# An attention and expert kernel: expert layers on two batches at once by seven block products in place of eight, with all weight conversion in the first two batches

## The chip, the cores and the metric

One core of a Trainium2 chip. The time is the device time of one execution in microseconds (us). The kernel before has a median of 1721.91 us over 3 runs (1719.16 to 1723.12).

## What is computed

Attention with a mixing of the heads ahead of the softmax and behind it, then four matrix products per token ("experts"); 8 batches, 12 heads, 448 positions, head size 64:

```python
scores = scale * np.matmul(q, k.transpose(0, 1, 3, 2))
scores = np.einsum('bhij,hg->bgij', scores, w_pre)
attn = softmax(scores)
attn = np.einsum('bhij,hg->bgij', attn, w_post)
x = np.matmul(attn, v)            # as [8*448 tokens, 768]
a, b = x @ w1, x @ w2             # 768 -> 1024
out = ((a * b) @ w3) @ w_out      # 1024 -> 1024 -> 768
```

The four weights arrive as 64-bit floating-point words.

## The kernel before, in words

**Steps.** The program is written out as one loop over `n` from 0 to 365 (`run`, lines 526 to 591). A step is ten positions of a batch with all twelve heads, 120 rows of 448 scores; a batch is 45 steps, so that there are 360. Within a step, in this order: the load of the scores of step n+4 (`fetch`), what was put off from the step before (`do_later`: stores and weight loads on SP's one DMA queue), the softmax of n (`softmax`: a minimum `mn` on DVE, the exponential `e` on ACT), the scaling of the second mixing matrix for n-1 (`scale`, `w2` on DVE), the split of the scores of n+2 into a high part `rh` (DVE) and a low part `rl` (POOL), scores of the next batch (`qk`), the weight conversion, half of the step's share of expert matmuls (`advance`), the second mixing (`post`, tile `pso`, copied to `mt`), the product with v (`av`, tile `psa`), the other half, and the first mixing of n+1 (`mix`, tile `psm`).

**Two parts.** Operands of the split products are held in the type fp32r, and a product is made of three matmuls: high with high, high with low, low with high (`PAIRS`). Of every operand a high part is copied by ACT and a low part is made by POOL as the difference (`two_parts`, lines 101 to 104; `el` on line 386).

**Weights.** `converting` takes 72 pieces of 64-bit words (`cs`, 384 KB each), turns them into float32 by four DVE instructions and one of ACT (`to_f32`, lines 91 to 98) and splits them. First come 40 pieces of w_out and w3, whose product (`folding`, 384 matmuls into `psf`) is made in steps 16 to 48 and stored in `w34_d`; then 32 pieces of w1 and w2 (`unit_jobs`), which are used at once for batch 0 and stored in `w_d` for the others, 16 stores of 768 KB.

**Experts.** `expert_atoms` takes one batch: for each of 8 blocks of 128 columns and w1, w2 a group of 18 matmuls (line 373) into bank 6 or 7, their product on DVE (`em`), its two parts (`eh`, `el`), then 6 groups of 24 matmuls with the folded weight (line 398). That is 432 matmuls of 128 by 448 a batch and 3456 in all. They are given out to the steps by `shares`: 288 to steps 53 to 106, 432 to every 45 steps from there, the rest (739) behind the loop. Weights come as "units" of 768 or 512 KB, two ahead (`w_ahead`), seven ahead behind the loop. The attention output of a batch stays in SBUF, split into `xh` and `xl` straight from PSUM.

Of the kernel before, what the change touches and what calls it, by code (L numbers as in the profile page):

```python
# [16 lines left out]
IB = 10  # L17
# [3 lines left out]
GB = 15  # L21
# [4 lines left out]
LATE = 2 * NB + GB + 2  # L26
PAIRS = ((0, 0), (0, 1), (1, 0))

# [3 lines left out]
class Kernel:  # L32
# [52 lines left out]
    def to_f32(self, s, name):  # L85
# [11 lines left out]
        x = self.cs.tile([128, CW], F32, tag="x", name=f"cx{name}")[:, :n]  # L97
# [8 lines left out]
    def converting(self, jobs):  # L106


        words, made = [], None
        jobs = list(jobs)  # L110
        for n in range(-2, len(jobs) + 1):
            if n + 2 < len(jobs):
                src = jobs[n + 2][0]
                words.append(self.words(src, f"{self.n_words}"))
                self.n_words += 1
            if made:
                jobs[n - 1][1](made)
                made = None
            if 0 <= n < len(jobs):
                made = self.to_f32(words.pop(0), f"{self.n_made}")  # L120
                self.n_made += 1
            yield

# [102 lines left out]
    def post(self, n):  # L226
# [8 lines left out]
        copy = nc.scalar.copy if n < LATE else nc.vector.tensor_copy  # L235
# [16 lines left out]
    def av(self, b, a, g):  # L252
# [10 lines left out]
        if g % 3 == 2:  # L263
            if b not in self.xs:
                pool = self.xp[b % 2]
                self.xs[b] = [pool.tile([128, K1, S], F32R, tag=f"x{t}", name=f"x{t}{b}") for t in "hl"]
            h, l = (x[:, g - 2:g + 1, cols] for x in self.xs[b])
            q = self.psa[:, :, :W]
            self.ends.append((5, lambda: nc.scalar.copy(h, q)))
            self.soon.append((5, lambda: nc.vector.tensor_tensor(l, q, h.bitcast(F32), op=ALU.subtract)))  # L270
# [4 lines left out]
    def fold_jobs(self):  # L275
        self.fo = self.fp.tile([128, KF, 2, DM], F32R, tag="o", name="fo", bufs=1)
        for k in range(KF):
            for q in range(2):
                src = self.w_src[3][k * 128:(k + 1) * 128, 2 * q * DH:2 * (q + 1) * DH]
                hi, lo = (self.fo[:, k:k + 1, t, q * DH:(q + 1) * DH] for t in range(2))  # L280
                yield src.rearrange("p (a n) -> p a n", a=1), lambda x, hi=hi, lo=lo: self.two_parts(x, hi, lo)
        w3 = self.w_src[2].rearrange("(k p) f -> p k f", p=128)
        for f in range(KF):
            for k in (slice(0, 3), slice(3, 6), slice(6, 8)):
                yield w3[:, k, f * 256:(f + 1) * 256], lambda x, f=f, k=k: self.fold_part(x, f, k)
# [5 lines left out]

    def folding(self):
        nc = self.nc
        for f in range(KF):
            for half in range(2):
# [7 lines left out]
                z = self.fp.tile([128, 3, 2, 128], F32R, tag="z", name=f"fz{half}_{f}")  # L303
                q = p.rearrange("p (d c) -> p d c", c=128)
                dst = self.w34_d[half * 3:(half + 1) * 3, :, f].rearrange("d p t c -> p d (t c)")

                def low(z=z, q=q, dst=dst):
                    nc.vector.tensor_tensor(z[:, :, 1], q, z[:, :, 0].bitcast(F32), op=ALU.subtract)
                    self.later.append(lambda: nc.sync.dma_start(dst, z.rearrange("p d t c -> p d (t c)").bitcast(F32)))

                self.ends.append((6 + half, lambda z=z, q=q: nc.scalar.copy(z[:, :, 0], q)))
                self.soon.append((6 + half, low))
# [3 lines left out]
    def units(self):  # L316
        return [u for b in range(B) for u in
                [(w, f, 0) for f in range(KF) for w in range(2)] + [(3, d, q) for d in range(K1) for q in range(2)]]

    def load_unit(self):  # L320
        w, f, q = self.unit_list[self.n_loaded]
        t = self.wp.tile([128, K1, 2, 128], F32R, tag="w", name=f"wu{self.n_loaded}")
        if w < 2:
            self.nc.sync.dma_start(t.bitcast(F32), self.w_d[w][f])
        else:
            h = KF // 2
            t = t[:, :h]
            self.nc.sync.dma_start(t.bitcast(F32), self.w34_d[f][:, q * h:(q + 1) * h])
# [4 lines left out]
    def unit_jobs(self):  # L333

        h = K1 // 2
        for w, f, _ in self.unit_list[:2 * KF]:
            src = self.w_src[w].rearrange("(k p) f -> p k f", p=128)
            for q in range(2):
                yield src[:, q * h:(q + 1) * h, f * 256:(f + 1) * 256], lambda x, w=w, f=f, q=q: self.unit_part(x, w, f, q)

    def unit_part(self, x, w, f, q):
        h = K1 // 2
        if q == 0:
            self.unit = self.wp.tile([128, K1, 2, 128], F32R, tag="w", name=f"wu{self.n_loaded}")
            self.loaded.append(self.unit)
            self.n_loaded += 1
        t = self.unit
        self.two_parts(x, *(t[:, q * h:(q + 1) * h, i] for i in range(2)))
        if q:
            self.later.append(lambda: self.nc.sync.dma_start(self.w_d[w][f], t.bitcast(F32)))  # L350

    def next_unit(self):

        t = self.loaded.pop(0)
        while 2 * KF <= self.n_loaded + self.n_asked < len(self.unit_list) and \
                len(self.loaded) + self.n_asked < self.w_ahead:
            self.n_asked += 1
            self.later.append(self.load_unit)
        return t

    def experts(self):
        for b in range(B):
            yield from self.expert_atoms(b)

    def expert_atoms(self, b):
        nc, xs, hs = self.nc, self.xs.pop(b), []
        for f in range(KF):
            for i in range(2):
                w = self.next_unit()
                p = self.bank(6 + i, f"eg{b}_{f}_{i}")[:, :S]  # L370
                for k in range(K1):
                    for t, (x, y) in enumerate(PAIRS):
                        nc.tensor.matmul(p, w[:, k, x], xs[y][:, k],  # L373
                                         start=(k == 0 and t == 0), stop=(k == K1 - 1 and t == 2))
                        yield
                if i == 0:
                    a = self.sp.tile([128, S], F32, tag="a", name=f"ea{b}_{f}", bufs=1)
                    self.ends.append((6, lambda a=a, p=p: nc.scalar.copy(a, p)))
            m = self.sp.tile([128, S], F32, tag="m", name=f"em{b}_{f}", bufs=1)
            self.ends.append((7, lambda m=m, a=a, p=p: nc.vector.tensor_tensor(m, a, p, op=ALU.mult)))  # L380
            h = self.hp.tile([128, S], F32R, tag=f"h{f}", name=f"eh{b}_{f}")
            l = self.hp.tile([128, S], F32R, tag=f"l{f}", name=f"el{b}_{f}")

            def parts(m=m, h=h, l=l):
                nc.scalar.copy(h, m)  # L385
                nc.gpsimd.tensor_tensor(l, m, h.bitcast(F32), op=ALU.subtract)  # L386

            self.soon.append((None, parts))
            hs.append((h, l))
        self.do_ends()  # L390
        self.do_soon()
        for d in range(K1):
# [263 lines left out]
```

## Time and profile before

| what | value |
|---|---|
| median of 3 runs | 1721.91 us (1719.16 to 1723.12) |
| the profiled execution | 1720.68 us, its span 1718.9 us |
| TensorE (PE), busy | 1648.0 us, 96% |
| DVE, POOL, ACT, busy | 935.8, 752.0, 723.6 us |
| moved by DMA | 416.51 MB, 242 GB/s over the span |
| steps 0 to 19 | up to 122.4 us |
| steps 20 to 99 | 122.4 to 451.4 us |
| steps 100 to 358 | 451.4 to 1549.7 us |
| what is left | 1549.7 to 1718.9 us |

A step is counted from its first mixing (`psm`, line 199) on TensorE; the borders are the starts of those matmuls. PE's busy time counts the modelled ends of pipelined matmuls. ACT is ScalarE, DVE VectorE, POOL GpSimd; an idle time is named with what ended it.

### The profile page before, as it was taken

Reading aid. Unit: us, or ns where it says so; the run is one execution under the profiler, and the core shown is the slowest. Engines: PE = TensorE matmul, PEld = TensorE weight load, DVE = VectorE, ACT = ScalarE, POOL = GpSimd, SP = SyncE. Lnnn points to the kernel's source line nnn. Section 1 sums busy time; section 2 is a strip of 40 time slices with the busy share of each in tenths; the row PEclk is TensorE's granted clock in tenths of the full one; section 3 lists DMA queues with packets and bytes.
Section 4 is the critical chain, followed back from the end, with each engine's and each line's share of the span. In section 5 each row is a group of like instructions: output and inputs, shape, how many; then the busy total and the mean of one; then the engine's idle time right before and its main releaser. Section 6 shows DMA issues by size and latency. Waiting matters only on the chain.

```text
span 1718.9 us, 30630 instructions
## 1 busy us (share of the span) xinstructions
PE 1648.0 (96%) x10872; PEld 1487.2 (87%) x10872; DVE 935.8 (54%) x2502; ACT 723.6 (42%) x1734; POOL 752.0 (44%) x668
## 2 busy tenths in 40 slices
PE   3889998999999999999999999999999999999999
PEld 1579997788889999899989999899998999998998
DVE  4958667778745555455545555555555555552000
ACT  3867656667643443343433434334433322221010
POOL 1666555667643544444543445345544333231010
PEclk7999999999999999999999999999999999999999
DMA  7979768999888777787778877787768755765764
GB/s 258 294 251 288 244 216 257 289 302 293 265 245 273 241 243 225 240 264 244 247 219 264 253 234 235 246 257 248 244 214 269 226 190 174 236 192 219 263 203 130
DMA packets 186822, 416.51 MB, mean 242 GB/s; under 512 B 17582, under 2 KB 130990, under 8 KB 186670
## 3 DMA queue, kind: packets, MB, share of 16 engines
q1 hardware_dynamic: 186670, 414.57, 76.4%
q8 instruction: 85, 1.39, 0.3%
q14 instruction: 67, 0.55, 0.1%
HBM read 307.54 MB, written 106.95 MB: 241 GB/s over the span
## 4 chain that ended last, share of the span: by engine, by line
PE 72%; DMA 2%; DVE 1%; ACT 0%; issue 0%; POOL 0%; SPq 0%; DVEq 0%; ACTq 0%
PE eg L373 25%; PE eo L398 13%; PE pso L231 13%; PE psa L261 7%; PE psm L199 4%; PE psm L200 3%; PE psm L201 3%; PE psq L164 3%; PE psq L165 3%; DMA wu<-w_d 2%; DVE mn L208 0%; DVE cx L98 0%; DVE ca L95 0%; DVE ca L96 0%; ACT st L169 0%
## 5 line engine op out<-in xcount | busy, mean ns | idle before, releaser
L192 POOL TENSOR_TENSOR rl<-r,rh 120x448 fp32r<-120x448 f32 x360 | 413.2, 1148 | 697.4 <-DVE rh L191 330.5
L211 ACT ACTIVATE e<-psm,mn 120x448 f32<-120x448 f32 x360 | 228.5, 635 | 671.6 <-DVE sa L220 562.5
L373 PE MATMUL eg<-xh,wu 128*128 128x448 f32 x1536 | 478.4, 375 | 4.9 <-ACT wu L103 4.5
L208 DVE TENSOR_REDUCE mn<-psm 120x1 f32<-120x448 f32 x360 | 224.6, 624 | 422.5 <-PE psm L201 422.2
L231 PEld LDWEIGHTS pso<-w,e 120*112 120x112 f32 (+1 forms) x2880 | 348.0, 178 | 47.2 <-ACT mt L237 31.8
L231 PE MATMUL pso<-w,e 120*112 120x120 f32 (+1 forms) x2880 | 360.9, 268 | 15.9 <-ACT mt L237 14.9
L373 PEld LDWEIGHTS eg<-xh,wu 128*128 128x128 f32 x1536 | 284.1, 189 | 28.7 <-ACT wu L103 5.2
L373 PE MATMUL eg<-xl,wu 128*128 128x448 f32 x768 | 284.4, 370 | 0.0
L398 PE MATMUL eo<-eh,wu 128*128 128x448 f32 x768 | 233.9, 375 | 11.0 <-DMA wu<-w_d 11.0
L237 DVE COPY mt<-pso 112x480 f32<-112x480 f32 (+1 forms) x253 | 165.4, 654 | 137.3 <-PE pso L231 136.4
L169 ACT COPY st<-psq 112x448 f32<-112x448 f32 x336 | 173.1, 526 | 16.2 <-DMA raw_d<-st 13.2
L398 PEld LDWEIGHTS eo<-eh,wu 128*128 128x128 f32 x768 | 143.2, 190 | 23.6 <-DMA wu<-w_d 12.9
L261 PE MATMUL psa<-mt,v 112*64 112x150 f32 (+1 forms) x2304 | 156.9, 292 | 1.9 <-DVE xl L270 1.3
L199 PE MATMUL psm<-rh,wph 120*120 120x448 f32 x360 | 139.6, 388 | 18.1 <-DVE rh L191 18.1
L373 PEld LDWEIGHTS eg<-xl,wu 128*128 128x128 f32 x768 | 145.0, 189 | 11.0 <-issue 0.2
L261 PEld LDWEIGHTS psa<-mt,v 112*64 112x64 f32 x2304 | 143.6, 137 | 7.8 <-DVE xl L270 1.6
L191 DVE CAST rh<-r 120x448 fp32r<-120x448 f32 x360 | 146.0, 406 | 0.4 <-DMA r<-raw_d 0.4
L398 PE MATMUL eo<-el,wu 128*128 128x448 f32 x384 | 142.9, 372 | 0.0
L201 PE MATMUL psm<-rl,wph 120*120 120x448 f32 x360 | 132.7, 369 | 0.3 <-POOL rl L192 0.2
L200 PE MATMUL psm<-rh,wpl 120*120 120x448 f32 x360 | 132.5, 368 | 0.0
L386 POOL TENSOR_TENSOR el<-em,eh 128x448 fp32r<-128x448 f32 x64 | 73.8, 1153 | 129.5 <-ACT eh L385 129.5
L164 PE MATMUL psq<-kk,qh 128*112 128x448 f32 x336 | 124.7, 371 | 3.3 <-ACT st L169 3.0
(51 smaller groups left out, 1900.9 us busy)
## 6 DMA issues: line engine op xcount, KB each, us to landing
wu<-w_d SPq DMA_DIRECT2D x112, 768.0 KB, 5.9
r<-raw_d SPq DMA_DIRECT2D x352, 210.0 KB, 3.3
raw_d<-st SPq DMA_DIRECT2D x168, 392.0 KB, 4.1
wu<-w_d SPq DMA_DIRECT2D x96, 512.0 KB, 5.4
v<-v SPq DMA_DIRECT2D x144, 224.0 KB, 4.9
kq<-kq SPq DMA_DIRECT2D x42, 672.0 KB, 7.1
cs<-w SPq DMA_DIRECT2D x32, 384.0 KB, 6.5
w_d<-wu SPq DMA_DIRECT2D x16, 768.0 KB, 5.6
```

The lines of the kernel that those rows point to most:

```text
L164: nc.tensor.matmul(p, qh[:, cols], kk, start=True, stop=False)
L169: copy(st[:, c % 2], p)
L192: nc.gpsimd.tensor_tensor(rl[:K], r[:K], rh[:K].bitcast(F32), op=ALU.subtract)
L199: nc.tensor.matmul(p[:K, :S], self.wph[:K, :K], rh[:K], start=True, stop=False)
L200: nc.tensor.matmul(p[:K, :S], self.wpl[:K, :K], rh[:K], start=False, stop=False)
L201: nc.tensor.matmul(p[:K, :S], self.wph[:K, :K], rl[:K], start=False, stop=True)
L208: nc.vector.tensor_reduce(mn[:K], p[:K, :S], axis=AX.X, op=ALU.min)
L211: nc.scalar.activation(e[:K], p[:K, :S], AF.Exp, bias=mn[:K], scale=-1.0, accum_out=sm[:K])
L231: nc.tensor.matmul(p[:, j, :, :w], e[:K, j * JT:(j + 1) * JT], w2[:K, :, :w], start=True, stop=True)
L261: nc.tensor.matmul(self.psa[rows, g % 3, :W], v[:, j, rows], mt[:, j, 2 * g + s, :W], start=(j == 0), stop=(j == NJ - 1))
L373: nc.tensor.matmul(p, w[:, k, x], xs[y][:, k], start=(k == 0 and t == 0), stop=(k == K1 - 1 and t == 2))
L398: nc.tensor.matmul(p, w[:, k % (KF // 2), x], hs[k][y], start=(k == 0 and t == 0), stop=(k == KF - 1 and t == 2))
```

## The change

Two batches 2p and 2p+1 are taken as one problem. The operand is cut into quarters: 11 and 21 are the upper and lower half of the features of the first batch, 12 and 22 of the second. Instead of eight products of a weight quarter with an operand quarter there are seven products of sums (Strassen's scheme in the form with the fewest additions), numbered 1 to 7 and made in the order 1, 6, 7, 5, 3, 2, 4.

- A pair has 11 groups of columns. Of w1 and w2 there are 8 groups of 9 matmuls, of the folded weight 3 groups of 12, each seven times: 756 matmuls a pair, 3024 in all.
- The weight sums are made once: for each of 12 sets of four quarters POOL does four additions or subtractions (`quarter`, 48 in all), and the seven results are split (ACT and POOL) in a `g` buffer and stored, 84 stores of 384 KB (`staged`). `do_micro` lets at most three of these pieces go into a step.
- The pieces of w1 and w2 are now taken alternately with those of w3, and all 72 are done by about step 90. Folding is spread over steps 22 to 91. No expert matmul runs before step 103; pair p is worked on in the 90 steps from 90(p+1)+13, the last pair behind the loop.
- The attention output goes from PSUM through ACT to DRAM (`x_d`, 48 stores) and comes back as quarters in float32 (96 loads of 224 KB). Operand sums are subtractions on DVE (`prepare`), 40 a pair; each product's operands are split by ACT and POOL, 70 splits a pair where there were 16 for two batches.
- Results are gathered from PSUM by one ACT copy and seven DVE additions per group (`gather`). The product a*b moves from DVE to POOL (`mult`, 64 in all). All `mt` copies are ACT's; before, DVE made those of steps from 107 on.
- Units are 384 or 512 KB, three ahead.

The core of the diff:

```diff
-LATE = 2 * NB + GB + 2
+NS = 51
+ORDER = (1, 6, 7, 5, 3, 2, 4)
...
+    def quarter(self, name, have, q, x, new, put):
+        def part(product, x):
+            self.micro.append(lambda: put(product, x))
+        def add(out, a, b, op):
+            self.micro.append(lambda: self.nc.gpsimd.tensor_tensor(out, a, b, op=op))
...
+    def staged(self, x, name, store):
+        if self.n_staged > 2:
+            self.do_later()
+        t = self.zp.tile([128, 3, 2, 128], F32R, tag="g", name=name, bufs=4)
+        self.two_parts(x, t[:, :, 0], t[:, :, 1])
...
-        copy = nc.scalar.copy if n < LATE else nc.vector.tensor_copy
+        copy = nc.scalar.copy
...
-            self.ends.append((5, lambda: nc.scalar.copy(h, q)))
-            self.soon.append((5, lambda: nc.vector.tensor_tensor(l, q, h.bitcast(F32), op=ALU.subtract)))
+            def leave():
+                nc.scalar.copy(x, q)
+                self.later.append(store)
+            def store():
+                nc.sync.dma_start(dst, x)
...
+            def split():
+                hi, lo = (self.take(f"{p}{name}_{m}_{k}", F32R) for p in ("eh", "el"))
+                nc.scalar.copy(hi, x)
+                nc.gpsimd.tensor_tensor(lo, x, hi.bitcast(F32), op=ALU.subtract)
...
+                if to:
+                    nc.vector.tensor_tensor(a[out], a[to[0]], p, op=ALU.add)
+                else:
+                    nc.scalar.copy(a[out], p)
...
+                def mult():
+                    x, y = acc[f, 0][q], acc[f, 1][q]
+                    nc.gpsimd.tensor_tensor(x, x, y, op=ALU.mult)
...
+            for k in range(nk):
+                for t, (x, y) in enumerate(PAIRS):
+                    nc.tensor.matmul(p, w[:, k, x], ops[m, k][y],
+                                     start=(k == 0 and t == 0), stop=(k == nk - 1 and t == 2))
...
-        FOLD, SWITCH, E_AT = 16, NB + 5, NB + 8
-        E_1, E_2 = 2 * KF * K1 * 3, K1 * KF * 3
+        FOLD, F_END, SWITCH = GB + 7, 2 * NB + 2, 2 * NB + 7
+        E_1 = 7 * 3 * (2 * K1 // 2 * KF // 2 + KF // 2 * K1 // 2)
...
-        share = shares(FOLD, SWITCH - 1, F_N) | shares(E_AT, LATE, E_1)
-        for n in range(LATE, N - 1, NB):
-            share |= shares(n, min(n + NB, N), int((E_1 + E_2) * min(1, (N - n) / NB)))
+        share = shares(FOLD, F_END, F_N)
+        for pair in range(B // 2 - 1):
+            first = 2 * NB * (pair + 1) + 13
+            last = min(first + 2 * NB, N + 6)
+            share |= shares(first, last, E_1 if last < N else E_1 - 60)
...
+            self.do_micro(3)
```

What stands on POOL in the second batch, in the kernel before: each `rl` is one step; `wu` is the low part of a piece of w1 or w2, `ql` and `kk` are the low parts of q and k.

```order
L192 TENSOR_TENSOR rl_5096<-r_4968,rh_5095 120x448
L104 TENSOR_TENSOR wu_5045<-cx_5054,wu_5045 128x3x128
L192 TENSOR_TENSOR rl_5154<-r_5021,rh_5153 120x448
L104 TENSOR_TENSOR wu_5164<-cx_5118,wu_5164 128x3x128
L192 TENSOR_TENSOR rl_5205<-r_5072,rh_5204 120x448
```

The same engine in the second batch after the change; `cx` and `fz` on the left are sums of weight quarters, `g` and `gz` low parts of a product's weight, `fw` that of a piece of w3.

```order
L243 TENSOR_TENSOR rl_3573<-r_3440,rh_3572 120x448
L136 TENSOR_TENSOR cx_3349<-cx_3415,cx_3349 128x384
L112 TENSOR_TENSOR g_2_6_3592<-cx_3349,g_2_6_3592 128x3x128
L112 TENSOR_TENSOR g_2_2_3595<-cx_3524,g_2_2_3595 128x3x128
L205 TENSOR_TENSOR ql_6_3619<-kq_3_3377,qh_6_3618 128x448
L206 TENSOR_TENSOR kk_6_3620<-kq_3_3377,kk_6_3620 64x448
L243 TENSOR_TENSOR rl_3637<-r_3499,rh_3636 120x448
L136 TENSOR_TENSOR cx_3524<-cx_3524,cx_3349 128x384
L112 TENSOR_TENSOR g_2_3_3645<-cx_3524,g_2_3_3645 128x3x128
L243 TENSOR_TENSOR rl_3684<-r_3556,rh_3683 120x448
```

Where one low part stood between two `rl`, there are up to five other instructions.

POOL again, in the fourth batch, before; `el` is the low part of an expert operand.

```order
L192 TENSOR_TENSOR rl_9705<-r_9583,rh_9704 120x448
L386 TENSOR_TENSOR el_0_9667<-em_0_9665,eh_0_9666 128x448
L154 TENSOR_TENSOR ql_1_9746<-kq_0_9355,qh_1_9745 128x448
L155 TENSOR_TENSOR kk_1_9747<-kq_0_9355,kk_1_9747 64x448
L192 TENSOR_TENSOR rl_9764<-r_9640,rh_9763 120x448
L192 TENSOR_TENSOR rl_9810<-r_9689,rh_9809 120x448
L192 TENSOR_TENSOR rl_9861<-r_9738,rh_9860 120x448
```

And there after the change:

```order
L243 TENSOR_TENSOR rl_9991<-r_9869,rh_9990 120x448
L511 TENSOR_TENSOR el0o_0_9995<-c_0_0_12_6389,eh0o_0_9994 128x448
L511 TENSOR_TENSOR el0o_1_9999<-c_1_0_12_6562,eh0o_1_9998 128x448
L205 TENSOR_TENSOR ql_1_10037<-kq_0_9628,qh_1_10036 128x448
L206 TENSOR_TENSOR kk_1_10038<-kq_0_9628,kk_1_10038 64x448
L243 TENSOR_TENSOR rl_10055<-r_9927,rh_10054 120x448
L511 TENSOR_TENSOR el0o_2_10059<-c_2_0_12_8076,eh0o_2_10058 128x448
L243 TENSOR_TENSOR rl_10103<-r_9975,rh_10102 120x448
L511 TENSOR_TENSOR el0o_3_10107<-c_3_0_12_8249,eh0o_3_10106 128x448
```

Expert low parts stand ahead of `rl` in nearly every step instead of in every third or fourth.

371 lines of the change are left out of this document (247 added, 124 removed).

## The prediction

> **What bounds the kernel now.** I read the page first, then the windows by stage, the chain of waits, the groups by line and the timeline at places where an engine waits. The page's first two parts:
>
> ```profile
> span 1718.9 us, 30630 instructions
> PE 1648.0 (96%) x10872; PEld 1487.2 (87%) x10872; DVE 935.8 (54%) x2502; ACT 723.6 (42%) x1734; POOL 752.0 (44%) x668
> PE   3889998999999999999999999999999999999999
> POOL 1666555667643544444543445345544333231010
> DMA  7979768999888777787778877787768755765764
> ```
>
> TensorE is nearly full from the eighth slice on, and the others have room there. In the first eight slices POOL, and above all the DMA engines (9 in three slices running), are far fuller than later. The same by stages, with borders at steps 20, 100 and 359; the columns are the stretch, its length, busy time (instructions) of PE, PEld, DVE, ACT, POOL, the granted clock, the DMA engines' share and GB/s:
>
> ```profile
> 0.00:122.40 122.40, 85.32 (x418) 53.71 (x419) 80.77 (x198) 73.96 (x171) 57.67 (x57) 0.87 0.84 270
> 122.40:451.40 329.00, 313.14 (x2197) 283.48 (x2196) 240.07 (x628) 219.76 (x522) 201.58 (x184) 0.99 0.87 268
> 451.40:1549.70 1098.30, 1086.71 (x7387) 1000.18 (x7386) 597.91 (x1647) 410.13 (x1005) 476.57 (x415) 1.00 0.76 237
> 1549.70:1718.90 169.20, 162.84 (x876) 149.82 (x874) 17.00 (x32) 19.73 (x37) 16.18 (x14) 1.00 0.61 207
> ```
>
> I call them A, B, C and D. C is PE's: 1086.7 of 1098.3 us. B is shared: PE 313 of 329, but DMA at 0.87, and in windows of 20 us inside B it is full:
>
> ```profile
> 306.00:326.00 20.00, 18.19 (x156) 16.04 (x156) 14.34 (x40) 14.12 (x35) 12.69 (x12) 1.00 1.03 303
> 358.00:378.00 20.00, 18.41 (x141) 16.26 (x140) 14.85 (x40) 13.26 (x32) 12.85 (x12) 1.00 1.00 325
> 390.00:410.00 20.00, 18.68 (x113) 16.29 (x113) 16.45 (x45) 15.84 (x39) 15.25 (x14) 1.00 1.02 336
> ```
>
> At a share of 1.00 to 1.03 they move 303 to 336 GB/s, 321 in the mean. That is the ceiling I use.
>
> The price of an expert matmul stands in the chain, where nothing else is on PE:
>
> ```profile
> 1627.95 58.24 PE eg L373 x288
> 1686.19 29.14 PE eo L398 x144
> ```
>
> 58.24 / 288 = 0.2022 us each. (The 375 ns that the groups show is the pipelined length.) So 3456 - 3024 = 432 fewer matmuls are worth 87 us of PE time. The question is in which stage they go, and what becomes late there.
>
> **What the change brings to the other engines.** Prices, from the groups by line (mean ns ahead of the last bar):
>
> ```profile
> L192 POOL TENSOR_TENSOR rl<-r,rh 120x448 fp32r<-120x448 f32 x360 | 413.2, 1148 | 697.4 <-DVE rh L191 330.5 <-issue 204.7 <-PE eo L398 32.5
> L191 DVE CAST rh<-r 120x448 fp32r<-120x448 f32 x360 | 146.0, 406 | 0.4 <-DMA r<-raw_d 0.4
> L223 DVE TENSOR_SCALAR w<-wpo,ri 120x120 f32<-120x120 f32 x360 | 120.0, 333 | 12.6
> L386 POOL TENSOR_TENSOR el<-em,eh 128x448 fp32r<-128x448 f32 x64 | 73.8, 1153 | 129.5 <-ACT eh L385 129.5
> L380 DVE TENSOR_TENSOR em<-ea,eg 128x448 f32<-128x448 f32 x64 | 39.4, 615 | 90.8 <-PE eg L373 90.6 <-POOL rl L192 0.3
> L104 POOL TENSOR_TENSOR wu<-cx,wu 128x384 fp32r<-128x384 f32 x32 | 32.3, 1008 | 0.4 <-DVE ca L96 0.4
> L103 ACT CAST wu<-cx 128x384 fp32r<-128x384 f32 x32 | 16.8, 525 | 0.0
> L237 ACT COPY mt<-pso 112x480 f32<-112x480 f32 (+1 forms) x107 | 61.4, 573 | 6.2 <-PE pso L231 6.1
> ```
>
> POOL's own time isn't all that it takes. Two places of the timeline, columns start and length:
>
> ```profile
> 408.61 0.28 DVE L223 TENSOR_SCALAR w<-wpo,ri 120x120 f32<-120x120 f32 x1
> 408.79 1.15 POOL L155 TENSOR_TENSOR kk<-kq,kk 64x448 fp32r<-64x448 f32 x1
> 409.12 1.06 DVE L191 CAST rh<-r 120x448 fp32r<-120x448 f32 x1 [0.23 <-DMA r<-raw_d]
> 463.44 1.00 POOL L104 TENSOR_TENSOR wu<-cx,wu 128x384 fp32r<-128x384 f32 x1
> 463.58 0.94 DVE L223 TENSOR_SCALAR w<-wpo,ri 120x120 f32<-120x120 f32 x1
> 464.40 1.17 POOL L154 TENSOR_TENSOR ql<-kq,qh 128x448 fp32r<-128x448 f32 x1
> 464.44 1.37 DVE L191 CAST rh<-r 120x448 fp32r<-120x448 f32 x1
> 465.64 1.18 POOL L155 TENSOR_TENSOR kk<-kq,kk 64x448 fp32r<-64x448 f32 x1
> ```
>
> The `w` of 0.28 us takes 0.94, and `rh` 1.06 and 1.37, when they start beside a POOL operation: they end just after POOL's does. So these two DVE instructions of every step and POOL exclude one another, and their 0.406 + 0.333 = 0.74 us a step count on POOL's account. Today this is rare, since POOL idles 697 us ahead of `rl`, 330 of them for that very `rh`. Between POOL operations there is also a gap of 0.07 us (465.64 less 464.40 + 1.17).
>
> **A, 122 us.** 40 fold matmuls leave steps 16 to 19; the rest stays. I take -3 us, between -7 (40 by 0.176, an estimate from 0.2022 by 384/448 columns) and 0.
>
> **B, 329 us.** PE loses 245 expert matmuls (50 us) and takes those 40 of folding (7 us): 313 - 43 = 270 us, so PE no longer binds. What does?
>
> DMA: 268 GB/s by 329 us is 88.2 MB. The queue's issues before:
>
> ```profile
> w_d<-wu SPq DMA_DIRECT2D x16, 768.0 KB, 5.6
> w_d<-fz SPq DMA_DIRECT2D x16, 384.0 KB, 4.3
> ```
>
> In place of 15 of the one (11.8 MB) and 16 of the other (6.3 MB) come 84 stores of 384 KB (33.0 MB), 11 stores and 9 loads of the attention output (4.6 MB) and 3 units (1.2 MB); one load of words fewer. That gives 108.5 MB, at 321 GB/s 338 us, at 336 and 303 GB/s 323 and 358 us. The old length is no longer to be had.
>
> POOL: 201.6 us before. To it come 84 low parts and 48 additions of 128 by 384 at 1.008 (133 us); 30 low parts `wu`, 6 `el` and one `fw` go (38 us): 296 us for 281 instructions. With 80 steps by 0.74 for `rh` and `w` (59 us) this is 355, with 281 gaps of 0.07 it is 375 us. ACT gains 84 - 30 copies at 0.525 and stays under 250 us. The load is uneven: by the order, POOL's own operations come to over 5 us a step in four of the sixteen stretches of five steps; taking in every stretch the larger of the two sums (DMA, POOL with its company), 391 us result. Bounds for B: 338 and 400. I take 378, near the even sum of POOL, since its buffers smooth part of the unevenness: +49 us.
>
> **C, 1098 us.** By the order 2460 expert matmuls become 2156: 304 by 0.2022 is -61.5 us, and PE still has the largest sum, 1037. Cover is thin, though. POOL: 476.6 before, 156 more `el` by 1.153 and 46 products by 1.148 on top, 707 us; with 259 steps by 0.74 and 611 gaps 941 us, 91% of 1037. ACT takes over 244 copies of `mt` at 0.573 and 156 splits at about 0.55, 410 + 226 = 636 us: not bound. DVE gives up those copies and gets 77 additions a pair of about 0.615: unchanged. A gain is also possible here: PE waits for late units of the folded weight. The row of the waits (us in total, times, longest), one of the places, and the window behind it:
>
> ```profile
> PE eo L398 <- DMA wu<-w_d: 11.0, 5, 2.6
> 505.71 0.74 PE L398 MATMUL eo<-eh,wu 128*128 128x448 f32 x1 [2.52 <-DMA wu<-w_d]
> 505.70:509.00 3.30, 3.29 (x13) 3.13 (x14) 0.54 (x1) 0.00 (x0) 1.60 (x2) 0.52 1.07 287
> ```
>
> 11 us of waiting, and behind a wait of 2.5 us about 3.3 us at a clock of 0.52, which loses 1.6: with three of those some 16 us. Units are now asked for 27 matmuls ahead and not 24, so such waits may go or may come at the 24 operand loads of every pair. I leave them as they are, and add 15 us for `rl` coming late: one POOL operation (1.15) in every twentieth step of 259. C: -47, between -77 (waits gone, nothing new) and 0.
>
> The page GPSIMD Engine Reference of the Trainium skill, Specifications, says that POOL shares its SBUF interfaces with DVE not only for such fast modes but also for DVE instructions with two SBUF inputs. The rows above agree for the modes; no run here shows the other, for want of such an instruction. By it the 92 subtractions on operands that fall into C would add 92 by about 0.6, 55 us (an estimate with the row of `em`), and 996 us would stand against PE's 1037, which makes the second rival below likelier.
>
> **D, 169 us.** 751 matmuls behind step 359 become 868: 117 by 0.2022 is +23.7. The chain of subtraction, copy and low part at three layer changes may cost one POOL operation each, 3 us. D: +27, between +23 and +40. Weights keep their rate (128 KB for three matmuls), and with 0.61 of DMA taken today the operand loads fit.
>
> **Sum.** -3 + 49 - 47 + 27 = +26 us on a span of 1718.9: 1744.9. The execution lasted 1.8 us longer than its span (1720.68), and the median of the runs is 1.2 us above it: 1748 us. So the matmuls are saved, but half of them are saved where PE no longer sets the pace.
>
> **Rivals.** *Conversion only as long as its bytes (faster).* If POOL's exclusions cost little and DMA alone sets B, B is 338 us (+9), and if the late units also go, C is -77: -3 + 9 - 77 + 24 = -47, so 1675 us; with the waits left as they are, 1690. For it: there is no stretch of the old trace in which POOL is near full. Against: the three sums of B must then overlap without loss. It decides in B: at about 352 us the whole comes out even. Chance 0.22.
> The page DMA: Bandwidth & Descriptors of the Trainium skill, Where 436 GB/s comes from, puts the limit of such transfers at 358 GB/s; the full windows here stay at 303 to 336. By its figure B's bytes would take 303 us, an estimate that would make this rival likelier.
>
> *POOL sets the pace in C too (slower still).* POOL with its company has 91% of PE's time on average but more in batches with `ql` and `kk`; if lateness of `rl` eats the gain, C is 0 and B 391: -3 + 62 + 0 + 30 = +89, 1811 us. For it: `el` stands ahead of `rl` in nearly every step. Against: `rl` is made two steps ahead. Chance 0.15.
>
> *The change cancels out.* B at 352 with C at -47, within 0.2% of before (about what a measurement can tell here): chance 0.07. That the matmuls don't fall is excluded: the order counts 3024.
>
> **Chances and range.** Forecast 0.56, the rivals as given: faster 0.22, same 0.07, slower 0.71. The range leaves out the outer part of both rivals: 1695 to 1800 us.
>
> **What would show it.** Right: steps 20 to 99 last about 378 us with a DMA share over 0.9, POOL about 300 us busy in them, and `rh` and `w` with means well over 0.406 and 0.333; steps 100 to 358 last about 1050 us. Wrong: B under 350 us, or a C over 1090 us with PE waiting on `rl`, or idle stretches of PE behind the loop.

## The result, and the profile after

The changed kernel takes 1808.78 us (median of 4 runs, 1806.63 to 1811.67) against 1721.61 us for the kernel before on the same chip: a ratio of 1.0509 [1.0487, 1.0531]. It is slower, as forecast, but by 87 us instead of 26, and 9 us outside the range. The profiled execution has a span of 1809.5 us, 90.6 more than before. The page's first parts:

```profile
span 1809.5 us, 31868 instructions
PE 1628.6 (90%) x10440; PEld 1453.7 (80%) x10440; DVE 1105.9 (61%) x2565; ACT 957.8 (53%) x2211; POOL 1191.7 (66%) x1048
PE   4887868778769999999999999999999999998999
POOL 2657686877756765777666776777656656744665
PEclk7987988988979999999999999999999999999999
DMA  7889788888677897877988888878988766668785
```

From the fourth slice to the twelfth, about the stage B and the switch behind it, PE stands at 6 to 8 where it had 8 or 9; its granted clock is down too, and nothing else is full either: POOL 5 to 8, DMA 6 to 9. The windows by stage show the same, with the columns of the prediction; the third row is the switch (steps 100 to 102), so rows three and four together are the stage C:

```profile
0.00:121.70 121.70, 85.34 (x379) 51.02 (x379) 78.64 (x192) 71.87 (x165) 55.49 (x55) 0.82 0.84 269
121.70:529.40 407.70, 312.09 (x1993) 277.46 (x1992) 242.84 (x604) 240.02 (x571) 297.34 (x283) 0.88 0.82 262
529.40:549.50 20.10, 11.39 (x43) 8.57 (x41) 6.11 (x16) 7.42 (x17) 7.07 (x8) 0.58 0.94 301
549.50:1608.60 1059.10, 1029.95 (x7045) 942.66 (x7044) 684.19 (x1615) 589.00 (x1362) 718.00 (x610) 0.99 0.80 249
1608.60:1809.50 200.90, 189.81 (x992) 174.01 (x990) 94.15 (x139) 49.51 (x97) 113.76 (x96) 0.97 0.76 241
```

| stage | before | forecast of the difference | after | difference |
|---|---|---|---|---|
| A, steps 0 to 19 | 122.4 | -3 | 121.7 | -0.7 |
| B, steps 20 to 99 | 329.0 | +49 | 407.7 | +78.7 |
| C, steps 100 to 358 | 1098.3 | -47 | 1079.2 | -19.1 |
| D, the rest | 169.2 | +27 | 200.9 | +31.7 |
| span | 1718.9 | +26 | 1809.5 | +90.6 |

In B every load came out as worked out: POOL 297.3 us in 283 instructions (forecast 296 in 281), ACT 240 (under 250), 262 GB/s by 407.7 us = 106.8 MB (108.5). The stage is longer than each of these sums and than all bounds given for it. So none of these sums sets it. The waits in B (us in total, times, longest), first after, then what stood there before:

```profile
PE pso L282 <- ACT mt L288: 86.1, 38, 8.4
ACT g L111 <- POOL cx L136: 55.9, 24, 4.0
ACT gz L111 <- POOL fz L136: 22.0, 9, 3.6
```

```profile
PE pso L231 <- ACT mt L237: 10.5, 18, 1.5
```

PE waits for ACT's copy `mt`, which empties the one PSUM bank of `pso`: 86 us instead of 10. ACT, for its part, waits 78 us for sums (`cx`, `fz`) that POOL is still making; before, it had no such wait. A place of the timeline, ACT, POOL and PE's `pso` alone (start, length, and in brackets the idle time ahead and who ended it):

```profile
253.31 1.13 POOL L243 TENSOR_TENSOR rl<-r,rh 120x448 fp32r<-120x448 f32 x1
254.40 1.06 POOL L112 TENSOR_TENSOR fw<-cx,fw 128x384 fp32r<-128x384 f32 x1
255.42 1.15 POOL L136 TENSOR_TENSOR fz<-fz,fz 128x384 f32<-128x384 f32 x1
256.60 0.51 ACT L111 CAST gz<-fz 128x384 fp32r<-128x384 f32 x1 [3.61 <-POOL fz L136]
257.02 0.56 ACT L288 COPY mt<-pso 112x480 f32<-112x480 f32 x1
257.63 1.94 PE L282 MATMUL pso<-w,e 120*112 120x120 f32 x8 [3.98 <-ACT mt L288]
```

The sum `fz` stands third in POOL's queue. ACT's first instruction of the split, `gz`, stands at once behind it in the program, so ACT is held 3.6 us; `mt`, 0.56 us of work whose input has long been there, stands behind `gz`; PE waits 4.0 us for `mt`. That is the chain sum, split, `mt`, `pso` over three queues that each work in order.

### The profile page after: what moved, and what is told of

It reads as the page before. It is cut to its first block, busy times and chain, and to the rows that moved or that the text cites. A ratio compares the mean times of both kernels' runs of the same rounds, so it can differ in the third digit from the quotient of the medians.

```text
span 1809.5 us, 31868 instructions
## 1 busy us (share of the span) xinstructions
PE 1628.6 (90%) x10440; PEld 1453.7 (80%) x10440; DVE 1105.9 (61%) x2565; ACT 957.8 (53%) x2211; POOL 1191.7 (66%) x1048
## 5 line engine op out<-in xcount | busy, mean ns | idle before, releaser
L282 PEld LDWEIGHTS pso<-w,e 120*112 120x112 f32 (+1 forms) x2880 | 364.4, 186 | 136.9 <-ACT mt L288 121.8
L569 PE MATMUL e<-eh,wu 128*128 128x448 f32 x1344 | 417.6, 377 | 24.5 <-DVE c2o L525 4.7
L569 PEld LDWEIGHTS e<-eh,wu 128*128 128x128 f32 x1344 | 252.5, 191 | 50.4 <-DVE c L525 6.9
L569 PE MATMUL e<-el,wu 128*128 128x448 f32 x672 | 253.4, 377 | 2.5 <-POOL el L511 2.5
L288 ACT COPY mt<-pso 112x480 f32<-112x480 f32 x360 | 205.9, 572 | 51.0 <-PE pso L282 49.8
L242 DVE CAST rh<-r 120x448 fp32r<-120x448 f32 x360 | 188.9, 525 | 12.4 <-DMA r<-raw_d 10.3
L525 DVE TENSOR_TENSOR c<-c,e 128x448 f32<-128x448 f32 x224 | 135.1, 615 | 69.8 <-PE e L569 65.2
L274 DVE TENSOR_SCALAR w<-wpo,ri 120x120 f32<-120x120 f32 x360 | 163.6, 454 | 12.6
L511 POOL TENSOR_TENSOR el<-x,eh 128x448 fp32r<-128x448 f32 x120 | 136.5, 1153 | 9.6 <-ACT eh L510 9.6
L569 PEld LDWEIGHTS e<-el,wu 128*128 128x128 f32 x672 | 129.0, 192 | 11.7 <-POOL el L511 2.9
L205 POOL TENSOR_TENSOR ql<-kq,qh 128x448 fp32r<-128x448 f32 x84 | 96.6, 1150 | 54.7 <-ACT qh L203 53.4
```

The lines of the kernel that those rows point to most:

```text
L242: nc.vector.tensor_copy(rh[:K], r[:K])
L274: nc.vector.tensor_scalar_mul(w2[:K, :, :w], wv[:K, :, :w], ri[:K])
L282: nc.tensor.matmul(p[:, j, :, :w], e[:K, j * JT:(j + 1) * JT], w2[:K, :, :w], start=True, stop=True)
L288: self.ends.append((4, lambda: copy(dst, p[:, :, :, :w])))
L511: nc.gpsimd.tensor_tensor(lo, x, hi.bitcast(F32), op=ALU.subtract)
L569: nc.tensor.matmul(p, w[:, k, x], ops[m, k][y], start=(k == 0 and t == 0), stop=(k == nk - 1 and t == 2))
```

## The experiments

Four theories were in play from here: W, the waits just shown; D, DMA's bytes; S, POOL's load with DVE excluded beside it; P, for the stage C, operand subtractions on DVE in front of the gathers for which PE waits. Times are medians; stage lengths below are from the traces, one execution of each kernel, with the same step borders. How far single executions differ can be seen where kernels share a stage's program: the five with the order of flow have B between 362.9 and 366.4 us, and the six with the splits of switch_split_later have 1047.8 to 1056.0 for steps 103 to 358. A few us in a stage of one execution therefore say little. Line numbers differ a little from kernel to kernel.

**late_split.** The split of a product's weight is issued one step after its sum, so that ACT should find the sum made.

```
-            self.micro.append(lambda: put(product, x))
+            self.micro.append(lambda: self.parts_due.append((x, lambda: put(product, x))))
...
     def do_micro(self, count):
+        self.do_parts()
```

> Only the place of the splits moves: a product's weight is split one step after the step in which POOL made its sum; the work and the bytes stay. Stage B (steps 20 to 99) takes 408 us now. Theory W (ACT works in order and stands 97 us at high-part copies for which POOL has not yet made the sum; the copies of mt behind them come late, TensorE waits 86 us for them, and its clock halves after each wait): ACT's waits on the sums go, B falls to about 350 us and the whole to about 1750 us. Theory S (POOL's own load with the DVE instructions that it excludes sets B): B stays within 10 us of 408. Theory D (DMA bytes set B): no change either.

1782.45 us, 1.0353 [1.0334, 1.0373]; B 382.2 us, 25.5 less than in the changed kernel with the same work and bytes, where W had expected about 350. Four waits of PE of 7 to 10 us remained, all where a sum overwrites a quarter whose split is still due, so that sums and splits alternate within one step. One of them:

```profile
362.45 1.00 POOL L139 TENSOR_TENSOR cx<-cx,cx 128x384 f32<-128x384 f32 x1
363.48 0.92 ACT L111 CAST g<-cx 128x384 fp32r<-128x384 f32 x2 [2.62 <-POOL cx L139]
364.07 1.96 POOL L112 TENSOR_TENSOR g<-cx,g 128x384 fp32r<-128x384 f32 x2 [0.62 <-ACT g L111]
...
367.42 0.51 ACT L111 CAST g<-cx 128x384 fp32r<-128x384 f32 x1 [3.01 <-DMA w_d<-g]
367.83 0.56 ACT L301 COPY mt<-pso 112x480 f32<-112x480 f32 x1
...
368.44 1.94 PE L295 MATMUL pso<-w,e 120*112 120x120 f32 x8 [7.96 <-ACT mt L301]
```

In this place and one other of the four, the last wait of a split, here 3.0 us, was ended by a store (`w_d<-g`) that freed one of the four `g` buffers.

**mt_on_dve.** The copies `mt` of steps 0 to 96 go to DVE.

```
-        copy = nc.scalar.copy
+        copy = nc.vector.tensor_copy if n < 2 * NB + 7 else nc.scalar.copy
```

> The copies of mt of steps 0 to 96 go from ACT to DVE, which is busy 243 of B's 408 us; sums and splits stay as they are. W: ACT still waits for the sums, but no copy that TensorE needs stands behind them any more; TensorE's waits for mt in B (86 us) mostly go, B falls to 350 to 370 us, the whole to about 1765 us. S and D: POOL's load and the bytes are the same, B stays within 10 us of 408, or gets longer by DVE's new load (77 copies by 0.65 us).

1809.49 us, 1.0519 [1.0496, 1.0542]; B 399.0, A 6 us longer. W's 350 to 370 for B was missed, and what S and D expected came. ACT's waits stay, and PE's wait changes its engine, since DVE too is fed by ACT: at the longest of these waits (5.2 us) ACT's `cm` stands behind a split that waits 3.7 us for its sum, DVE waits 6.1 us for `cm` with its `cx`, and `mt` stands behind `cx`. The waits in B:

```profile
PE pso L282 <- DVE mt L288: 67.5, 47, 5.2
ACT g L111 <- POOL cx L136: 62.7, 23, 4.4
DVE cx L106 <- ACT cm L99: 24.7, 16, 6.1
```

**no_sums.** The 48 sums of weights are left out; splits and stores go on with the unsummed quarters.

```
-            self.micro.append(lambda: self.nc.gpsimd.tensor_tensor(out, a, b, op=op))
+            pass
```

> The 48 sums of weight quarters are left out (each product takes a quarter as it is, so the output is not the product wanted); the splits and stores of all 84 stay. W: as late_split, B about 345 us, since both the waits and 48 us of POOL go. S: POOL loses 48 operations of 1.0 us and B falls by about 50 us to 358. D: B stays near 408. Read together with late_split: what this run gains beyond it is POOL's load.

1765.05 us, 1.0253 [1.0233, 1.0274]; B 361.1, POOL busy 250.6 us there. Without sums POOL has 47 us less to do, and ACT no sum to wait for. The splits wait for stores to free `g` buffers instead, and PE still waits for `mt`. This run alone doesn't tell W from S. The waits in B:

```profile
PE pso L282 <- ACT mt L288: 54.3, 39, 6.7
ACT g L111 <- DMA w_d<-g: 22.2, 8, 5.0
```

**stores_twice.** Each of the 84 product stores is made a second time, to another place: 33 MB more in B.

```
             store(t.bitcast(F32))
+            self.nc.sync.dma_start(self.twice_d[self.n_twice % 28], t.rearrange("p k t c -> p (k t c)").bitcast(F32))
```

> Every one of the 84 stores of product weights is made a second time to a place that nobody reads: 33 MB more, at 321 GB/s 103 us of all DMA engines, nearly all of it in stage B. D: B goes from 408 to about 490 us or more. W and S: DMA has a share of 0.82 in B and room for about 75 us; B grows by 20 to 40 us, to 430 to 450 us.

1823.78 us, 1.0594 [1.0573, 1.0616]; B 418.4, 10.7 us more for 33 MB. The window of B:

```profile
119.50:537.90 418.40, 317.68 (x1993) 280.27 (x1992) 243.63 (x604) 240.31 (x571) 297.32 (x283) 0.87 0.97 334
```

334 GB/s held over 418 us: the prediction's 321 was no ceiling, and B of the changed kernel isn't bound by bytes.

**flow.** As late_split, but at most two splits a step, a sum pulls out only the split of the quarter that it overwrites, and a new set of quarters pushes out only older pieces of its own kind, not all.

```
-        while self.micro and count > 0:
-            self.micro.pop(0)()
+        for _ in range(min(2, len(self.parts_due))):
+            self.parts_due.pop(0)[2]()
+        while self.micro and count > 0 and len(self.parts_due) < 3:
+            self.micro.pop(0)[1]()
...
-            self.do_micro(99)
+            self.do_older("z")
```

> As late_split (382 us in B, the whole 1782), and besides at most two splits go into a step, and a new set of quarters pushes out only older pieces of its own kind, so that no step has a run of sum, split, sum, split. Theory W (TensorE waits because ACT, in order, stands at such runs: three waits of 8 to 10 us are left in B of late_split): those waits go, B falls to about 360 us and the whole to 1760. Theory S (POOL's load sets B): POOL has the same work, B stays at 382 or above.

1766.32 us, 1.0264 [1.0227, 1.03]; B 364.4, 43 less. The window of B and its two main waits:

```profile
119.40:483.80 364.40, 293.13 (x1993) 254.61 (x1992) 265.28 (x604) 239.47 (x571) 297.46 (x283) 0.93 0.90 292
PE pso L307 <- ACT mt L313: 58.6, 40, 6.7
ACT g L111 <- POOL cx L138: 17.4, 12, 5.4
```

The same 283 instructions on POOL in the same 297 us, in another order: this shows that the order costs 43 of B's 79 us, as W has it; S, by which B would have stayed at 382 or above, fell. Of the 43, 19.0 are busy time of PE, whose 1993 matmuls run at a higher clock, and 24.3 are idle time; the wait for `mt` falls from 86.1 to 58.6 us.

**fold_twice.** Each folding group is computed twice over (384 matmuls more, nearly all in B), to see whether PE or its halved clock sets B.

```
-                for k in range(KF):
+                for k in [*range(KF), *range(KF)]:
```

> The kernel after the change, but each of the 16 folding groups is made twice, the first pass being overwritten: 384 more matmuls of 128 by 384, 68 us of TensorE at full clock, spread over steps 22 to 91. Theory K (TensorE isn't the bound of B; it idles 2 to 4 us at a time, and runs 99 of 408 us at half clock because of that): with less idling the clock holds, half clock falls below 50 us and B grows by less than 20 us or even shrinks. Rival (TensorE at its real clock is the bound of B): B grows by 60 us or more.

1809.64 us, 1.0511 [1.0464, 1.0558]. The window of B:

```profile
119.20:529.40 410.20, 353.79 (x2378) 325.74 (x2376) 242.88 (x604) 239.63 (x571) 298.38 (x283) 0.95 0.82 261
```

PE is busy 353.8 us instead of 312.1 and the stage is 2.5 us longer. The time at half clock falls from 99 to 44 us. So PE's own work doesn't set B: 42 us more of it fit into its idle time. What the clock alone costs this run doesn't show, since the matmuls added may have taken what the clock gave back.

**no_subs.** The 40 subtractions on operands of each pair are left out; the products take unsubtracted operands.

```
-                sub(b[12][k], b[12][k], b[11][k])
-                x = t2[k] = self.take(f"t{name}_{k}")
-                sub(x, b[22][k], b[12][k])
+                x = b[22][k]
```

> The 40 operand subtractions of each pair are left out (products take operand quarters as they are, so the output is not the product wanted); splits, gathers and loads stay. Theory P (a subtraction with two SBUF inputs takes up to 1.57 us on DVE beside a POOL operation, four or more come at once at a layer change, and the gathers for which TensorE waits stand behind them): the waits of 2.5 to 4 us per layer and the half clock behind them go, steps 103 to 358 fall from 1059 to about 1035 us, and what lies behind step 359 by 5 us. Rival (late units or operand loads make those waits): steps 103 to 358 stay within 5 us.

1771.11 us, 1.0287 [1.0248, 1.0326]; steps 103 to 358 take 1027.4 us, 32 less, D 7 less. Why, the changed kernel's timeline shows at a layer change (DVE, POOL and PE, with cuts):

```profile
928.47 1.18 POOL L206 TENSOR_TENSOR kk<-kq,kk 64x448 fp32r<-64x448 f32 x1
928.56 1.56 DVE L481 TENSOR_TENSOR x<-x,x 128x448 f32<-128x448 f32 x1
...
929.72 1.39 POOL L243 TENSOR_TENSOR rl<-r,rh 120x448 fp32r<-120x448 f32 x1
930.16 1.43 DVE L481 TENSOR_TENSOR t<-x,x 128x448 f32<-128x448 f32 x1
931.51 0.61 DVE L481 TENSOR_TENSOR x<-x,x 128x448 f32<-128x448 f32 x1
...
932.16 0.62 DVE L481 TENSOR_TENSOR t<-x,x 128x448 f32<-128x448 f32 x1
...
932.70 0.61 DVE L525 TENSOR_TENSOR c0o<-c0o,e0o 128x448 f32<-128x448 f32 x1
...
933.37 0.74 PE L569 MATMUL e<-eh,wu 128*128 128x448 f32 x1 [4.16 <-DVE c0o L525]
```

Beside POOL a subtraction of 0.61 us takes 1.43 to 1.56; four subtractions stand on DVE ahead of the gather `c0o`, and PE waits 4.2 us for it. In steps 103 to 358 PE's waits for gathers come to 16.3 us; without the subtractions 0.2 are left. Behind the wait of 4.2 us the window from 933.30 to 936.70 runs at half clock:

```profile
933.30:936.70 3.40, 3.33 (x9) 2.89 (x10) 1.38 (x7) 0.79 (x4) 1.58 (x2) 0.50 1.04 376
```

This agrees with the rule of the Trainium skill, GPSIMD Engine Reference, Specifications, that the prediction could not check: DVE contends with POOL also with two SBUF inputs. The prediction's estimate by that rule was 55 us on POOL's account; leaving the subtractions out made these steps 32 us shorter.

**mult_on_dve.** The 64 products a*b go from POOL to DVE.

```
-                    nc.gpsimd.tensor_tensor(x, x, y, op=ALU.mult)
+                    nc.vector.tensor_tensor(x, x, y, op=ALU.mult)
```

> The 64 products a*b go from POOL back to DVE. POOL loses 77 us in all, 55 of them in steps 103 to 358. If POOL's load (718 of 1059 us there) delays rl and so TensorE, these steps get 10 to 25 us shorter. Theory P (DVE's queue, with two-input operations that POOL excludes, is what delays the gathers): they stay, or get longer by up to 10 us.

1809.37 us, 1.0509 [1.046, 1.0559]; C as in the changed kernel (1061.4 for steps 103 to 358) with 43 us less on POOL and 13 more on DVE. So less load on POOL brought nothing. The products on DVE may have taken back a gain, but in the changed kernel PE has no wait for `rl` in these steps either.

**switch_later.** As flow, with the first operands of the paired products prepared three steps later.

```
-            if n == SWITCH + 2:
+            if n == SWITCH + 5:
```

> The kernel flow with the first operand preparation at the switch to the paired products set back by three steps, so that its loads and its copies no longer stand in ACT's queue in front of the last copies of the weights' pieces. Theory that the switch's 20 us for three steps (10 before the change) come from ACT standing at loads just issued: the switch takes about 11 us, the rest as in flow, about 1755 us in all. Rival, that the leftover pieces of the weights cost this time, or that it is only moved to the steps behind: 1763 to 1768 us, as flow.

1770.87 us, 1.0276 [1.0243, 1.0309]; the switch takes 22.1 us, as in flow (22.7). The theory that ACT stands at loads just issued fell.

**switch_subs_pool.** As switch_later, with the operand subtractions on POOL.

```
-                nc.vector.tensor_tensor(out, x, y, op=ALU.subtract)
+                nc.gpsimd.tensor_tensor(out, x, y, op=ALU.subtract)
```

> The kernel switch_later with the 40 operand subtractions of each pair on POOL instead of DVE. If C is long because these subtractions stand on DVE, slowed by POOL, in front of gathers for which PE waits, C's steps 103 to 358 lose 15 to 30 us of their 1060 and the rest 3 to 7 of its 199, as when they were left out (32 and 7): about 1725 to 1740 us. Rival, that POOL, busy 718 us of C in the changed kernel, then has some 40 us more and is late with rl and the operand's low parts: C no shorter or longer, 1755 us or above.

1820.21 us, 1.0565 [1.0541, 1.059]; steps 103 to 358 take 1082.4 (+21), D 228.4 (+30). The rival's side, but its reason isn't the one given: no wait for `rl` leads the list. The old chain is back in C, with ACT's copies `eh` of the operands standing for POOL:

```profile
ACT eh L535 <- POOL t L506: 48.9, 26, 4.8
PE pso L307 <- ACT mt L313: 24.7, 12, 5.4
```

**switch_split_later.** As switch_later, with each operand's split one step after its subtraction.

```
-            self.soon.append((None, split))
+            self.later.append(split)
```

> The kernel switch_later with each operand sum's split into two parts issued one step after the sum, as late_split does for the weights. If ACT's wait for the sums (52 us in C of the changed kernel) is what holds PE there, C loses about as much as it did in the weights' stage for such waits, 15 us or more: 1740 us or below. If the gathers behind the subtractions on DVE are what PE waits for, nothing changes: 1753 to 1758 us, as switch_later.

1761.08 us, 1.0225 [1.0198, 1.0253]; steps 103 to 358 take 1047.8, 13 less, with 20 us at half clock in C instead of 41. That is a little less than the 15 us expected, and kernels with the same splits below have 1050.7 to 1056.0, so that the gain is rather 5 to 13 us; the 1740 us in all were not reached. The order of the splits matters in C too, but ACT's wait for the sums is not shown as the reason. In steps 103 to 358 ACT waited for `t` 1.8 us in the changed kernel (the 52 us of the expectation are of the whole execution, and 49.9 of them lie in D) and 3.0 in switch_later; with the later splits it waits more. First switch_later, then this kernel:

```profile
ACT eh L535 <- DVE t L506: 3.0, 3, 1.8
ACT eh L535 <- DVE t L506: 24.9, 28, 2.3
```

PE's idle time falls by 5 us and its busy time by 8. Why its waits became shorter was not settled. The trace also shows the switch:

```profile
482.64 4.13 SPq L502 DMA_DIRECT2D x<-x_d  x9
...
486.87 0.45 SPq L260 DMA_DIRECT2D r<-raw_d  x1
...
493.60 0.39 DVE L267 CAST rh<-r 120x448 fp32r<-120x448 f32 x1 [11.05 <-DMA r<-raw_d]
...
494.04 0.73 PE L275 MATMUL psm<-rh,wph 120*120 120x448 f32 x1 [9.02 <-DVE rh L267]
```

Nine operand loads are issued ahead of the next rows of scores, `r`, on the same queue; DVE waits 11 us for these rows and PE 9 us for DVE. In the changed kernel DVE waits 9.5 us for them at this place.

**loads_apart.** As switch_split_later, with three of the nine loads at the switch, behind the first units, and six five steps later.

```
-        for f in phases[0][0] + phases[1][0]:
-            f()
+        for f in phases[0][0]:
+            self.later.append(f)
...
+        for f in phases[1][0]:
+            self.later.append(f)
```

> The kernel switch_split_later with the paired products' first operands loaded in two lots, three behind the weights' first units at the switch and six five steps later, instead of nine at once ahead of the next rows of scores. If DVE's 11 us wait for these rows behind the operands' bytes is what makes the switch's three steps take 22 us, they take 11 to 15 us, about 1750 to 1755 us in all. Rival, that the wait only moves to the steps behind: 1759 to 1763 us.

1756.13 us, 1.0202 [1.0176, 1.0227]; the switch takes 13.7 us instead of 22.6 (few_stores, with the same loads: 14.6). That was its cause. The whole gained 5 us; steps 103 to 358 took 1052.9 instead of 1047.8, which lies within what single executions differ by. This is the fastest version of the change with all of its work in, and still about 2% slower than the kernel before.

**sums_at_end.** As switch_split_later, with the step's sums and splits behind `mt`.

```
-            self.do_micro(3)
...
             self.do_ends()
+            self.do_micro(3)
```

> The kernel switch_split_later with the step's sums and splits of weights issued at the end of the step, behind ACT's copy mt, instead of ahead of the step's second folding share. If what is left in the conversion stage is the ring of one step (PE's scores, DVE's minimum, ACT's exponential, its copies, mt, PE's pso), then the splits' copies (0.5 us each, about one in a step) leave it for the time in which ACT waits for DVE's minimum (55 us there): the stage takes 335 to 350 us instead of 363, about 1735 to 1748 us in all. Rival, that POOL's load sets what is left: 360 to 365 us, 1758 to 1763 us in all.

1771.0 us, 1.027 [1.0231, 1.0309]; B 372.3, 9 more. The wait for `mt` falls to 34.5 us (56.4 in switch_split_later), but one for POOL's `rl` comes up, on whose queue the sums now stand ahead of it:

```profile
PE pso L307 <- ACT mt L313: 34.5, 28, 7.5
PEld psm L277 <- POOL rl L268: 27.8, 21, 3.8
```

My theory of one step's ring fell: taken out of ACT's way, the sums are in POOL's.

**sums_at_end_none.** The same without the 48 sums (splits and stores of unsummed quarters).

```
-            self.micro.append((name, now))
+            pass
```

> The kernel sums_at_end with the 48 sums of weights left out (the splits and stores go on with unsummed blocks). If POOL's load or DVE's waiting beside it sets what is left of the conversion stage, the stage gets 15 to 30 us shorter than in sums_at_end. If the ring of one step sets it, less than 8 us.

1740.14 us, 1.0108 [1.008, 1.0136]; B 345.8, 26.5 less than sums_at_end. So in that order the sums cost 26.5 us of B, within the 15 to 30 that S expected. Whether by POOL's 46 us of work or by ACT's 35 us of waiting for it, this run doesn't tell: both go with the sums.

**few_stores.** As loads_apart without the stores of products 5, 6 and 7; their units are loaded from products 1, 2 and 3.

```
-                self.staged(x, f"gz{c}_{product}", lambda t: nc.sync.dma_start(
+                self.staged(x, f"gz{c}_{product}", lambda t: product < 5 and nc.sync.dma_start(
...
-            src = self.w_d[w][f][m - 1]
+            src = self.w_d[w][f][(m - 1) % 4]
```

> The kernel loads_apart without the stores of products 5, 6 and 7 (36 of 84, 14 MB less in the conversion stage); their units are loaded from products 1, 2 and 3, all splits stay. If bytes set what is left of the stage once the order is mended, 14 MB at 334 GB/s (stores_twice) are up to 42 us: the stage takes 325 to 350 us instead of 365. If they don't, it takes 358 to 367 us, 1749 to 1758 us in all.

1750.11 us, 1.0159 [1.0137, 1.0182]; B 361.4, 4.1 less for 14 MB, hardly more than single executions differ by. In the mended order bytes don't bind B either.

**few_stores_no_sums.** As sums_at_end_none (no sums) without the same stores.

> The kernel sums_at_end_none (no sums of weights) without the same 36 stores. If its DMA share of 0.95 is what holds the stage at 346 us, it takes 325 to 338 us, near the 329 before the change. If the remaining copies and low parts in the ring of one step hold it, it stays at 341 us or above.

1732.36 us, 1.0057 [1.0035, 1.0079]; B 338.0, 7.8 less. With the sums out, the stores begin to count, by their bytes or by the `g` buffers that they hold: ACT's waits for free ones fall from 9.3 to 1.6 us. 9 us over the 329 of before remain; what holds them was not settled.

## Why the prediction was wrong, step by step

**B, the step that failed.** "Taking in every stretch the larger of the two sums" measured the stage by loads, and of ACT it said only that it "stays under 250 us". The loads themselves came out right, and no sum of them sets the stage. What was not priced is what the change adds between the queues: 84 splits, 48 of which wait, with their first half on ACT, for a sum on POOL, with `mt` behind it on ACT, and PE behind `mt`. With that order mended and nothing else (flow) B is 364 us: 43 of the 79 us were the order. The other 36 are less than the +49 of the forecast, so its sum of POOL with exclusions (375) and its 391 were too high: the exclusions are there, as foretold (see below), but not all on the path. Of the 36, the runs put 26.5 on the sums and 8 on the stores, each in an order of its own (sums_at_end), so these needn't add up in flow; how the 36 divide there stays open.

The sign that the prediction named for B catches this: it asked for a DMA share over 0.9, and it is 0.82. The part on `rh` and `w` held:

```profile
L242 DVE CAST rh<-r 120x448 fp32r<-120x448 f32 x360 | 188.9, 525 | 12.4 <-DMA r<-raw_d 10.3 <-POOL el L511 2.1
L274 DVE TENSOR_SCALAR w<-wpo,ri 120x120 f32<-120x120 f32 x360 | 163.6, 454 | 12.6
```

Their means rose from 406 and 333 ns. POOL excludes DVE; the exclusions just aren't what PE waits for most in B.

**C, the matmuls right, two terms put at nothing.** The matmuls fell by 299 (304 foretold), 60.5 us at 0.2022. PE busy fell by 45.4 only (1086.7 to 11.39 + 1029.95): 15 us went to the clock, at half for 44 us instead of 10. PE's idle time rose by 26 (11.6 to 37.9). -60.5 + 15 + 26 is the -19 measured. The forecast allowed 15 us for these, for `rl` coming late, which isn't what came. What came: the switch (10 us, operand loads ahead of the rows of scores, by loads_apart), for which the forecast had no term; and DVE, foretold as "unchanged" from the copies that it gives up and the additions that it gets. Those additions have the 0.615 us foretold, but the subtractions are missing from that sum (the prediction has them on POOL's account alone, 92 by about 0.6): 116 fall into C, with means of 0.86 to 1.45 us by group, 125 us together, and DVE's busy time rose from 597.9 to 690.3. They stand ahead of gathers for which PE waits (no_subs: 32 us, though in that run POOL, too, is 21 us less busy there). Issuing their splits later gave back 5 to 13 us, part of the same 32 (switch_split_later). The waits for late units, left as they were in the forecast, fell from 11.0 to 3.8 us.

**D, +32 for +27.** 992 - 876 = 116 matmuls by 0.2022 are 23.5 us, as foretold. 4.7 us of idle time came on top (6.4 to 11.1), and 11 us at half clock can account for the rest, 3.5. **A** came out 2.3 us above its forecast, within its bounds.

**The rivals.** POOL setting the pace in C did not happen (C is 19 us shorter, no wait for `rl`, and mult_on_dve), though the time came near the one given for it (1811): the same total, by another way. The bytes rival fell by stores_twice. The forecast's sign and its reason, that matmuls are saved where PE no longer sets the pace, held. The range was too narrow because no case had a price for a wait between queues in B. Slips in the working without weight: a folding matmul by its ratio is 0.173 us and not 0.176, and C's POOL terms as listed give 709 us in 617 instructions and not 707 in 611 (measured: 725 in 617). The 321 GB/s called a ceiling was none (stores_twice: 334).

## What to carry to other kernels

When a change adds a pair of operations on two engines that work in order, the second waiting for the first, list what stands behind the second on its queue and who waits for that; a sum of busy time can't show it. Here the same work cost 43 us less in flow, with the second issued a step later and, as a rule, at most two of them in a step. Count a mended order as part of the change before judging the idea: with it the blocked scheme lost 2% instead of 5%, and still lost.

## What the runs showed of the hardware

In the changed kernel's trace the stretches of TensorE at half clock last 3.4 us or a multiple of it, but for the one that the end cuts off. Waits of PE shorter than 3.4 us bring such a stretch: in steps 103 to 358 PE has eight waits of 2.5 us or more, seven of them under 3.4, and near the end of seven of the eight, six of these under 3.4, a stretch at half clock begins. Behind this one of 2.5 us the clock over the next 3.4 us was 0.55.

```profile
676.17 0.71 PE L569 MATMUL e<-eh,wu 128*128 128x448 f32 x1 [2.51 <-DVE w L274]
676.10:679.50 3.40, 3.33 (x14) 3.12 (x15) 3.37 (x5) 0.00 (x0) 2.69 (x2) 0.55 0.88 266
```

The Trainium skill, TensorE: Matmul & The Clock Gate, Part 1, has the clock fall after at least one idle window of about 3.4 us; here less was enough.

DVE's subtractions with two SBUF inputs, 0.61 us alone, took up to 1.59 us beside POOL; the gather's additions of the same size, whose second input lies in PSUM, kept a mean of 0.615. And mixed transfers with every store made twice ran at 334 GB/s over 418 us.
